# Four heads' numerators in four adjacent PSUM banks, one multiply for qT, whole loads, and stores placed behind loads

## The chip, the cores and the metric

The kernel runs on one core of one Trainium2 chip. The metric is the time of one execution in microseconds (us) on the device; lower is better. A program on one core gives runs that differ by one to two per cent, so each comparison below ran both kernels in the same rounds on the same chip. A run counts as fast unless it is over 1.5% above the fastest run of its own kernel. The profiles are of single executions; times in them are us from the start of the span.

## The reference, cut to what matters

```python
q_p = phi(q)              # relu(q) * cos and relu(q) * sin, side by side: 64 -> 128 features
k_p = phi(k)
kv  = einsum('bhsf,bhsd->bhfd', k_p, v);   z = sum(k_p, axis=2)
num = einsum('bhsf,bhfd->bhsd', q_p, kv);  den = einsum('bhsf,bhf->bhs', q_p, z)[..., None] + 1e-06
x   = num / den                            # 8 batches, 8 heads, 576 positions, 64 wide; heads joined to 512
wq, wk = x @ w_q, x @ w_k                  # 512 -> 64
mixed  = (wq @ wk.T / 8) @ x
out    = relu(mixed) @ w_out               # fp32, 8 x 576 x 512
```

## The kernel before

Heads are worked in 16 groups of four (H = 0 to 15), two groups to a batch. For each group TensorE does `qT` (transposes of relu(q)), `kv`, `num` (numerator, with the denominator as a 65th column) and `xT` (transposes of x). For each batch it does `wqk`, `wk`, `kx` and four `mx`. For each pair of batches it does nine row tiles `wo` of the output, each copied out by `oe` and stored by `st` in five stores of one or two tiles. VectorE multiplies k by cos and sin (`mk`, line 392), does the qT multiply (`qe`, line 420) and the division (`norm`). POOL does most of the ReLUs and casts of inputs (`rq`, `rk`, `rv`). `plan_order` simulates the engines once on the host and fixes the order of all operations; each engine then works in that order, and so does each queue that issues transfers. The plan also holds TensorE back once in every 256 of its instructions, and longer when the transfers are behind (the variables `left_in` and `block`).

```python
def norm(H, r, m):                       # twice for a group: r = 0, 1
    nv = bank(m, 2)[:, :, 0:SC * (D + 1)].rearrange("p t (u e) -> p t u e", u=SC)
    ...
    nc.vector.reciprocal(rec, nv[:, :, :, D:D + 1])
    ...
    nc.vector.tensor_tensor(xv[:, h, r], nv[:, :, :, 0:D], rec.to_broadcast([P, 2, SC, D]), op=ALU.mult)
...
def qT_evac(H, r, m):                    # twice for a group
    nc.vector.tensor_mul(qpt_bufs[H % 2][:, r, :, D:SLOTS * D],
        bank_h(m)[:, 0:1, 0:HC].to_broadcast([P, 2, HC]), cst)
...
CS = ((0, 5), (5, C9))                   # a tile of inputs is loaded in two parts
    if kind == "load":
        load(j, parts=CS, names=(b,))
    ...
    elif kind == "st":                   # a store is two transfers, each of 64 partitions
        last = b == B // 2 - 1 and j >= 2
        store(b, j, (nc.sync, A if last else nc.sync))
...
for n, eng, m in plan_order(NB):
    emit(n, eng, m)
```

## Time and profile before

| | before |
|---|---|
| time, median of three runs (range) | 130.08 us (130.00 to 131.48) |
| span of the profiled run | 129.5 us (this run measured 131.6) |
| busy: TensorE, VectorE, ScalarE, POOL | 102.7, 95.0, 79.6, 71.1 us |
| first row tile starts, last copy ends | 44.3, 123.75 us |
| qT multiply of group 4, of group 15 starts | 28.4, 102.8 us |

The costliest rows of VectorE on the page (source line, engine, operation, output <- inputs, partitions x elements and type, count | busy us, mean ns of one | idle us just before, and what ended it) give the price of what is merged:

```profile
L466 DVE TENSOR_TENSOR x_sb<-ps,rec 128x640 bf16<-128x640 f32 x32 | 26.4, 825 | 1.1
L420 DVE TENSOR_TENSOR qpt_buf<-ps,cst 128x1152 bf16<-128x1152 bf16 x32 | 22.7, 750 | 1.7 <-PE ps L414 1.7
```

Thirty-two divisions of 640 elements and thirty-two qT multiplies of 1152 are 49.1 of VectorE's 95.0 us.

### The profile page before, as it was taken

The page shows a single profiled execution, that of the slowest core. Times are in us where ns is not written, and L with a number is a line of the kernel's source. Part 1 is how long each engine was busy: PE and PEld are TensorE (multiplying, and loading weights), DVE is VectorE, ACT ScalarE, POOL GpSimd, SP SyncE. Part 2 cuts the span into 40 slices and gives each one's busy share as a digit, 9 for nine tenths or more (in the row PEclk, how much of TensorE's full clock was granted, in tenths as well). Part 3 has the DMA queues.
Part 4 walks back from the last instruction along what each step waited for, and adds up shares of the span by engine and source line. Part 5 has one row for each costly group of instructions (what it writes and reads, how often), then busy time and mean ns, then how long its engine had stood idle before and what let it go on. Part 6 is the DMA issues. An engine that isn't in the chain of part 4 may idle for free.

```text
span 129.5 us, 5391 instructions
## 1 busy us (share of the span) xinstructions
PE 102.7 (79%) x2262; PEld 63.3 (49%) x2286; DVE 95.0 (73%) x156; ACT 79.6 (61%) x155; POOL 71.1 (55%) x113
## 2 busy tenths in 40 slices
PE   5957694757498998979997878998886999998900
PEld 2334353545375644646664645555564655543400
DVE  1067878999789999899989596999899688314000
ACT  6959435083705677687688755864766376656710
POOL 7720557568489999897289287876652710000000
PEclk9999999999756999999999999999999999999995
DMA  3999999999999999999999999999999754667893
GB/s 86 369 359 357 359 309 354 340 337 383 365 356 358 356 358 366 376 378 369 340 356 360 332 308 379 351 347 323 316 318 326 266 133 123 164 166 189 202 210 128
DMA packets 32968, 39.41 MB, mean 304 GB/s; under 512 B 3248, under 2 KB 27824, under 8 KB 32944
## 3 DMA queue, kind: packets, MB, share of 16 engines
q1 hardware_dynamic: 32304, 38.09, 90.9%
q10 hardware_dynamic: 640, 0.98, 2.6%
q8 instruction: 18, 0.29, 0.9%
q14 instruction: 6, 0.05, 0.1%
HBM read 29.62 MB, written 9.44 MB: 302 GB/s over the span
## 4 chain that ended last, share of the span: by engine, by line
PE 47%; DMA 19%; DVE 16%; issue 7%; ACT 3%; POOL 2%; SPq 1%; POOLq 0%
PE ps L563 20%; DMA raw<-in_k_dram 8%; PE ps L493 6%; DMA raw<-in_v_dram 6%; PE ps L453 4%; DVE qpt_buf L420 4%; PE ps L428 4%; DVE x_sb L466 4%; DMA raw<-in_q_dram 4%; DVE kp L392 3%; PE ps L478 3%; PE ps L523 3%; PE ps L539 2%; PE ps L414 2%; POOL rq_buf L379 2%
## 5 line engine op out<-in xcount | busy, mean ns | idle before, releaser
L563 PE MATMUL ps<-wo_sb,mix_sb 128*128 128x512 bf16 x126 | 34.4, 380 | 2.8 <-DVE xT_buf L368 0.9
L379 POOL TENSOR_SCALAR rq_buf<-raw 128x640 bf16<-128x640 f32 (+1 forms) x30 | 26.2, 887 | 16.9 <-DMA raw<-in_q_dram 13.5
L366 ACT COPY o_sb<-ps 128x512 f32<-128x512 f32 x36 | 21.1, 586 | 12.4 <-PE ps L563 11.0
L392 DVE TENSOR_TENSOR kp<-rk,cossin 128x2304 bf16<-128x2304 bf16 (+2 forms) x17 | 23.0, 1352 | 7.8 <-ACT rk L377 6.1
L466 DVE TENSOR_TENSOR x_sb<-ps,rec 128x640 bf16<-128x640 f32 x32 | 26.4, 825 | 1.1
L404 POOL TENSOR_SCALAR v_buf<-raw 128x640 bf16<-128x640 f32 (+1 forms) x26 | 22.5, 879 | 6.2 <-DMA raw<-in_v_dram 3.0
L420 DVE TENSOR_TENSOR qpt_buf<-ps,cst 128x1152 bf16<-128x1152 bf16 x32 | 22.7, 750 | 1.7 <-PE ps L414 1.7
L379 POOL TENSOR_SCALAR rk<-raw 128x640 bf16<-128x640 f32 (+1 forms) x28 | 18.3, 668 | 8.8 <-DMA raw<-in_k_dram 6.2
L563 PEld LDWEIGHTS <-mix_sb 128*128 128x128 bf16 x144 | 12.2, 97 | 14.5 <-issue 2.4
L428 PE MATMUL ps<-v_buf,kp 64*128 64x65 bf16 x576 | 13.1, 193 | 5.7 <-ACT v_buf L402 2.2
L428 PEld LDWEIGHTS <-kp 64*128 64x128 bf16 x576 | 11.1, 95 | 9.5 <-DVE kp L392 5.0
L453 PE MATMUL ps<-kv_sh,qpt_buf 64*128 64x65 bf16 x320 | 14.5, 193 | 1.2 <-issue 1.2
L551 ACT ACTIVATE mix_sb<-ps 128x576 bf16<-128x576 f32 x24 | 14.5, 655 | 1.4 <-PE ps L539 1.3
L453 PEld LDWEIGHTS <-qpt_buf 64*128 64x128 bf16 x640 | 12.9, 96 | 4.9 <-issue 3.9
L453 PE MATMUL ps<-kv_sb,qpt_buf 64*128 64x65 bf16 x320 | 14.5, 194 | 0.1
L368 DVE COPY xT_buf<-ps 128x640 bf16<-128x640 bf16 (+1 forms) x19 | 8.4, 456 | 6.1 <-PE ps L478 3.9
L289 PE MATMUL ps<-warm 128*128 128x512 bf16 x32 | 11.2, 487 | 1.8 <-DVE warm L285 1.5
L414 PE MATMUL ps<-ident,rq_buf 64*128 64x64 bf16 x288 | 8.3, 193 | 3.3 <-POOL rq_buf L379 1.8
L366 ACT CAST wT_buf<-ps 128x576 bf16<-128x576 f32 x8 | 5.1, 637 | 8.2 <-PE ps L493 8.2
L493 PE MATMUL ps<-xT_buf,wqk_sb 128*128 128x288 bf16 x64 | 10.1, 306 | 0.0
L366 ACT CAST kv_sb<-ps 128x260 bf16<-128x260 f32 x15 | 5.6, 375 | 6.9 <-PE ps L428 5.7
L478 PE MATMUL ps<-ident,x_sb 64*128 64x64 bf16 x288 | 7.6, 190 | 2.3 <-DVE x_sb L466 1.5
(51 smaller groups left out, 123.1 us busy)
## 6 DMA issues: line engine op xcount, KB each, us to landing
out_dram<-o_sb SPq DMA_DIRECT2D x30, 256.0 KB, 5.2
raw<-in_q_dram SPq DMA_DIRECT2D x16, 320.0 KB, 6.0
raw<-in_v_dram SPq DMA_DIRECT2D x16, 320.0 KB, 6.2
raw<-in_k_dram SPq DMA_DIRECT2D x15, 320.0 KB, 5.8
raw<-in_q_dram SPq DMA_DIRECT2D x16, 256.0 KB, 5.9
raw<-in_k_dram SPq DMA_DIRECT2D x16, 256.0 KB, 6.0
raw<-in_v_dram SPq DMA_DIRECT2D x16, 256.0 KB, 6.3
wo_f<-in_moe_w_out_dram SPq DMA_DIRECT2D x1, 1024.0 KB, 8.1
```

Source lines behind the costliest of these rows:

```text
L366: nc.scalar.copy(dst, src)
L379: eng.tensor_scalar(dst, src, FMAX, 0.0, op0=ALU.min, op1=ALU.max)
L392: nc.vector.tensor_mul(kp[H][:, 2 * lo:2 * hi], rks[H][:, lo:hi].rearrange("p c i d -> p (c i) d").unsqueeze(2) .to_broadcast([P, 2 * (hi ...
L404: eng.tensor_scalar(dst, src, 1.0, 1.0, op0=ALU.mult, op1=ALU.mult)
L420: nc.vector.tensor_mul(qpt_bufs[H % 2][:, r, :, D:SLOTS * D], bank_h(m)[:, 0:1, 0:HC].to_broadcast([P, 2, HC]), cst)
L428: nc.tensor.matmul(bank(m + r)[:, 0, i * (D + 1):(i + 1) * (D + 1)], kp[H][half_rows(r), 2 * c + i, :, :], v_bufs[H % 3][half_rows(r), c, ...
L453: nc.tensor.matmul(nb[t][:, u, :], qpt_bufs[H % 2][rows, r, w, u * P:(u + 1) * P], mv, start=(u == 0 and w == 0), stop=False)
L466: nc.vector.tensor_tensor(xv[:, h, r], nv[:, :, :, 0:D], rec.to_broadcast([P, 2, SC, D]), op=ALU.mult)
L478: nc.tensor.transpose(bank_h(m + r)[:, 0, k0 * D:(k0 + 1) * D], xs[b][half_rows(r), u, 2 * hp:2 * hp + 2, :], ident[half_rows(r), half_row ...
L493: nc.tensor.matmul(bank(m + nh)[:, 0, 0:hs], wqk_sb[:, dmc, :, :], xT_bufs[b % 2][:, dmc, nh * hs:(nh + 1) * hs], start=(dmc == 0), stop=( ...
L551: nc.scalar.activation(dst, src, AF.Relu, scale=scale_moe)
L563: nc.tensor.matmul(bank(m)[:, 0, :], mixs[bp][:, dmc, rt * P:(rt + 1) * P], wo_sb[:, dmc, :], start=(dmc == 0), stop=(dmc == NDM - 1))
```

## The change

Its intent: fewer and longer operations on VectorE, longer runs in the loads, stores that do not stand in front of loads, and more output buffers (12 for 5) so that row tiles never wait for a store. `plan_order` got new weights, so the whole order of the program moved too. The term `ds` puts every store 15 us later in the plan's list of transfers, and the last four row tiles are stored with their copies. The core of the diff, with cuts marked:

```diff
-PLAN = dict(mk=1.3, pa=7.848, ... wo_at=4, nraw=6, nout=5, ...)
+PLAN = dict(mk=1.3, pa=7.189, ... wo_at=3, nraw=6, nout=12, ... ds=15)
...
-                    key = t
+                    key = t + (par["ds"] if n[0] == "st" else 0)
...
-        for r in range(2):
-            op(("num", H, r), {"PE": .33}, [("kve", H), ("qe", H, r), ...], pa, "row", 2)
-            op(("norm", H, r), {"DVE": 1.0}, [("num", H, r)], 2, ...)
+        op(("num", H), {"PE": .68}, [("kve", H), ("qe", H), ...], par["pn"], "row", 4)
+        op(("norm", H), {"DVE": 1.68}, [("num", H)], par["pno"], ...)
...
-            qpt_bufs[H % 2][:, r, :, D:SLOTS * D],
-            bank_h(m)[:, 0:1, 0:HC].to_broadcast([P, 2, HC]), cst)
+            qpt_bufs[H % 2][:, :, :, D:SLOTS * D],
+            bank_h(m, 2)[:, :, 0:HC].unsqueeze(2).to_broadcast([P, 2, 2, HC]),
+            cst.unsqueeze(1).to_broadcast([P, 2, 2, HC]))
...
-    def norm(H, r, m):
+    def norm(H, m):
...
-        rec = small.tile([P, 2, SC, 1], FP32, name="rec")
+        rec = small.tile([P, 4, SC, 1], FP32, name="rec")
         nc.vector.reciprocal(rec, nv[:, :, :, D:D + 1])
...
-            xv[:, h, r], nv[:, :, :, 0:D], rec.to_broadcast([P, 2, SC, D]), op=ALU.mult)
+            xv[:, h], nv[:, :, :, 0:D], rec.to_broadcast([P, 4, SC, D]), op=ALU.mult)
...
-            load(j, parts=CS, names=(b,))
+            load(j, names=(b,))
...
             wout_evac(b, j, m, engs[eng])
+            if b == B // 2 - 1 and j > 4:
+                lo = (j - 5) % 2
+                store(b, (j + 1) // 2, (nc.sync, A), lo, lo + 1)
         elif kind == "st":
-            last = b == B // 2 - 1 and j >= 2
-            store(b, j, (nc.sync, A if last else nc.sync))
+            if b < B // 2 - 1 or j < 3:
+                store(b, j, (nc.sync, nc.sync))
```

More of the change, by code (lines that the diff above doesn't have):

```diff
@@ L22 @@
 EPS_HI = 9.9837780e-07
-PLAN = dict(mk=1.3, pa=7.848, pc=8.447, pm=8.738, pw=6.677, pb=0.821, flex=0.189, poe=11.845,
-            pme=34.049, pmk=1108.864, wo_at=4, nraw=6, nout=5, sw=0, amp=0, seed=99119,
-            sl=0.1, bd=0.2, pact=1)
+PLAN = dict(mk=1.3, pa=7.189, pc=7.595, pm=3.84, pw=4.572, pb=0.65, flex=0.147, poe=3714.738,
+            pme=7.206, pmk=16.167, wo_at=3, nraw=6, nout=12, sw=0, amp=0, seed=19615,
+            sl=0.05, bd=0.3, pact=1, pqe=92.894, pno=0.978, pn=7.389, res=0, ds=15)
 PAIRS = ((0, 1), (2, 3), (4,), (5, 6), (7, 8))
-PE_COUNT = dict(qT=36, kv=72, num=44, xT=36, wqk=16, wk=10, kx=20, mx=4, wo=8)
+PE_COUNT = dict(qT=36, kv=72, num=88, xT=36, wqk=16, wk=10, kx=20, mx=4, wo=8)
 def plan_order(NB, par=None):
@@ L48, in ago @@
         return name if cond else None
-    prep = {"POOL": 1.37, "ACT": 1.1} if par["pact"] else {"POOL": 1.37}
+    prep = {"POOL": 1.37, "ACT": 1.1}
     pa, pc, pm, pw = par["pa"], par["pc"], par["pm"], par["pw"]
@@ L63, in plan_order @@
                par["pmk"])
-        op(("qT", H), {"PE": .26}, [ago(H, "rq", H), ago(H, "kv", H - 1),
-                                    ago(H > 1, "num", H - 2, 1)], pa, "row", 2)
-        for r in range(2):
-            op(("qe", H, r), {"DVE": .67}, [("qT", H)], 3,
-               frees=(("qT", H), r))
+        op(("qT", H), {"PE": .26}, [ago(H, "rq", H), ago(H > 1, "num", H - 2)], pa, "row", 2)
+        op(("qe", H), {"DVE": 1.31}, [("qT", H)], par["pqe"], frees=(("qT", H), None))
         op(("kv", H), {"PE": .58}, [ago(H, "mk", H), ago(H, "rv", H),
-                                    ago(H > 2, "num", H - 3, 1)], pa, "row", 2)
+                                    ago(H > 2, "num", H - 3)], pa, "row", 2)
         op(("kve", H), {"ACT": .96, "DVE": 1.1}, [("kv", H)], 3,
            frees=(("kv", H), None))
-        for r in range(2):
-            op(("num", H, r), {"PE": .33}, [("kve", H), ("qe", H, r),
-                                        ago(b > 2, "kx", b - 3)], pa, "row", 2)
-            op(("norm", H, r), {"DVE": 1.0}, [("num", H, r)], 2,
-               frees=(("num", H, r), None))
-        op(("xT", H), {"PE": .24}, [("norm", H, 0), ("norm", H, 1),
-                                    ago(b > 1, "wqk", b - 2)], pc, "row", 2)
+        op(("num", H), {"PE": .68}, [("kve", H), ("qe", H), ago(b > 2, "kx", b - 3)],
+           par["pn"], "row", 4)
+        op(("norm", H), {"DVE": 1.68}, [("num", H)], par["pno"],
+           frees=(("num", H), None))
+        op(("xT", H), {"PE": .24}, [("norm", H), ago(b > 1, "wqk", b - 2)], pc, "row", 2)
         op(("xe", H, 0), {"ACT": .49, "DVE": .35}, [("xT", H)], 2, frees=(("xT", H), 0))
@@ L88, in plan_order @@
            frees=(("wqk", b), None))
-        op(("wqc", b), {"DVE": .36}, [("we", b)], 1)
+        op(("wqc", b), {"ACT": .57, "DVE": .36}, [("we", b)], 1)
         op(("wk", b), {"PE": .14}, [("we", b)], pc, "row", 1)
@@ L140, in plan_order @@
     while ready:
-        best = None
+        best, held = None, ()
+        for n in ready:
+            if ops[n]["banks"] == 4 and par["res"]:
+                u = min((0, 2, 4), key=lambda u: (sum(x > 1e8 for x in bank[u:u + 4]),
+                                                  max(bank[u:u + 4])))
+                held = range(u, u + 4)
         for n, t in ready.items():
@@ L151, in plan_order @@
                     s = max(free[e] + (.1 if o["mode"] != mode else 0), t)
-                    if o["banks"] == 2:
-                        u = min((0, 2, 4, 6), key=lambda i: max(bank[i], bank[i + 1]))
-                        s, mine = max(s, bank[u], bank[u + 1]), (u, u + 1)
-                    elif o["banks"] == 1:
-                        s = max(s, min(bank))
-                        u = max((i for i in range(8) if bank[i] <= s),
-                                key=lambda i: bank[i ^ 1])
-                        mine = (u,)
+                    w = o["banks"]
+                    where = [u for u in ((0, 2, 4) if w == 4 else range(0, 8, w))
+                             if w == 4 or u not in held]
+                    s = max(s, min(max(bank[u:u + w]) for u in where))
+                    u = max((u for u in where if max(bank[u:u + w]) <= s),
+                            key=lambda u: (bank[u ^ 1] if w == 1 else 0,
+                                           bank[(u ^ 2) & 6], u))
+                    mine = tuple(range(u, u + w))
                     key = s - .1 * o["prio"] + (par["sw"] if o["mode"] != mode else 0)
                 elif e == "DMA":
-                    key = t
+                    key = t + (par["ds"] if n[0] == "st" else 0)
                 elif len(o["cost"]) > 1:
@@ L417, in qT_mm, with qT_evac @@
                     ident[half_rows(r), half_rows(r)])
-    def qT_evac(H, r, m):
+    def qT_evac(H, m):
         nc.vector.tensor_mul(
-            qpt_bufs[H % 2][:, r, :, D:SLOTS * D],
-            bank_h(m)[:, 0:1, 0:HC].to_broadcast([P, 2, HC]), cst)
+            qpt_bufs[H % 2][:, :, :, D:SLOTS * D],
+            bank_h(m, 2)[:, :, 0:HC].unsqueeze(2).to_broadcast([P, 2, 2, HC]),
+            cst.unsqueeze(1).to_broadcast([P, 2, 2, HC]))
     def kv_mm(H, m):
@@ L441, in kv_evac, with num_mm @@
         kvs[H] = (kv_sb, kv_sh)
-    def num_mm(H, r, m):
-        nb = [bank(m + t)[:, 0, 0:SC * (D + 1)].rearrange(
-            "p (u e) -> p u e", u=SC) for t in range(2)]
+    def num_mm(H, m):
+        nb = [bank(m + j)[:, 0, 0:SC * (D + 1)].rearrange(
+            "p (u e) -> p u e", u=SC) for j in range(4)]
         kv_sb, kv_sh = kvs[H]
-        for u in range(SC):
-            for w in range(2):
-                for t in range(2):
-                    rows = half_rows(t)
-                    mv = (kv_sb[rows, r, t * (D + 1):(t + 1) * (D + 1)] if w == 0
-                          else kv_sh[rows, r, :])
-                    nc.tensor.matmul(
-                        nb[t][:, u, :], qpt_bufs[H % 2][rows, r, w, u * P:(u + 1) * P],
-                        mv, start=(u == 0 and w == 0), stop=False)
-        for t in range(2):
-            nc.tensor.matmul(nb[t][:, :, D], ones_t[half_rows(t), :],
-                             eps_t[half_rows(t), :], start=False, stop=True)
@@ L460, in norm @@
-    def norm(H, r, m):
+        for r in range(2):
+            for u in range(SC):
+                for w in range(2):
+                    for t in range(2):
+                        rows = half_rows(t)
+                        mv = (kv_sb[rows, r, t * (D + 1):(t + 1) * (D + 1)] if w == 0
+                              else kv_sh[rows, r, :])
+                        nc.tensor.matmul(
+                            nb[2 * t + r][:, u, :],
+                            qpt_bufs[H % 2][rows, r, w, u * P:(u + 1) * P],
+                            mv, start=(u == 0 and w == 0), stop=False)
@@ L461, in norm @@
+        for r in range(2):
+            for t in range(2):
+                nc.tensor.matmul(nb[2 * t + r][:, :, D], ones_t[half_rows(t), :],
+                                 eps_t[half_rows(t), :], start=False, stop=True)
+    def norm(H, m):
         b, h = divmod(H, 2)
-        nv = bank(m, 2)[:, :, 0:SC * (D + 1)].rearrange("p t (u e) -> p t u e", u=SC)
-        rec = small.tile([P, 2, SC, 1], FP32, name="rec")
+        nv = bank(m, 4)[:, :, 0:SC * (D + 1)].rearrange("p j (u e) -> p j u e", u=SC)
+        rec = small.tile([P, 4, SC, 1], FP32, name="rec")
@@ L464, in norm @@
         nc.vector.reciprocal(rec, nv[:, :, :, D:D + 1])
-        xv = xs[b].rearrange("p u (h t r) d -> p h r t u d", h=2, r=2)
+        xv = xs[b].rearrange("p u (h j) d -> p h j u d", h=2)
         nc.vector.tensor_tensor(
-            xv[:, h, r], nv[:, :, :, 0:D], rec.to_broadcast([P, 2, SC, D]), op=ALU.mult)
+            xv[:, h], nv[:, :, :, 0:D], rec.to_broadcast([P, 4, SC, D]), op=ALU.mult)
     def xT_mm(H, m):
@@ L500, in wqk_evac, with wq_copy @@
              bank(m, 2)[:, :, 0:hs])
-    def wq_copy(b):
+    def wq_copy(b, eng):
         wq2 = moe.tile([P, S], BF16, name="wq2")
-        nc.vector.tensor_copy(wq2[64:128], wT_bufs[b % 2][0:64, D:SLOTS * D])
+        copy(eng, wq2[64:128], wT_bufs[b % 2][0:64, D:SLOTS * D])
         wqTs[b] = wq2
@@ L571, in wout_evac, with store @@
         copy(eng, o_sbs[bp, g][:, rt - PAIRS[g][0], :], bank(m)[:, 0, :])
-    def store(bp, g, qs):
-        n = len(PAIRS[g])
-        for hi in range(2):
-            qs[hi].dma_start(
-                dataclasses.replace(out, offset=out.offset + out_dest(bp, PAIRS[g][0], hi),
-                                    ap=[[C9 * DM, 64], [2 * DM, n], [1, DM]]),
-                o_sbs[bp, g][64 * hi:64 * hi + 64, 0:n, :])
+    def store(bp, g, qs, lo=0, hi=2):
+        rts = PAIRS[g][lo:hi]
+        for half in range(2):
+            rows = slice(64 * half, 64 * half + 64)
+            qs[half].dma_start(
+                dataclasses.replace(out, offset=out.offset + out_dest(bp, rts[0], half),
+                                    ap=[[C9 * DM, 64], [2 * DM, len(rts)], [1, DM]]),
+                o_sbs[bp, g][rows, lo:lo + len(rts), :])
     A, V, G = nc.scalar, nc.vector, nc.gpsimd
@@ L604, in emit @@
         elif kind == "qe":
-            qT_evac(b, j, m)
+            qT_evac(b, m)
         elif kind == "kv":
@@ L610, in emit @@
         elif kind == "num":
-            num_mm(b, j, m)
+            num_mm(b, m)
         elif kind == "norm":
@@ L614, in emit @@
                 xs[b // 2] = xpool.tile([P, SC, NH, D], BF16, name="x_sb")
-            norm(b, j, m)
+            norm(b, m)
         elif kind == "xT":
@@ L624, in emit @@
         elif kind == "wqc":
-            wq_copy(b)
+            wq_copy(b, engs[eng])
         elif kind == "wk":
```

## The prediction

> **What bounds the kernel now.** I read the page's slices first, to see which engine is full when.
>
> ```profile
> PE   5957694757498998979997878998886999998900
> DVE  1067878999789999899989596999899688314000
> PEclk9999999999756999999999999999999999999995
> DMA  3999999999999999999999999999999754667893
> GB/s 86 369 359 357 359 309 354 340 337 383 365 356 358 356 358 366 376 378 369 340 356 360 332 308 379 351 347 323 316 318 326 266 133 123 164 166 189 202 210 128
> ```
>
> A slice is 3.24 us. The DMA engines are full from slice 1 to slice 30 (3 to 100 us) at about 355 GB/s. VectorE is at nine tenths from about 23 to 94 us. TensorE is half idle in the first third and at nine tenths after it. So the first 45 us are a problem of supply (loads, then VectorE), and the rest one of TensorE. The chain of waits agrees: up to 26.6 us it names only loads, from 28 to 62 us mostly VectorE, then TensorE almost alone. Its end:
>
> ```profile
> 113.92 0.65 PE ps L563 x3
> 114.57 0.25 PE ps L509 x5
> 114.82 0.97 PE ps L563 x4
> ...
> 118.66 4.49 PE ps L563 x20
> ...
> 123.17 0.58 ACT o_sb L366
> ```
>
> A row tile of the output product (line 563, four matmuls) costs 0.97 us. The last copy ends at 123.75 us, and the last store takes until 129.5, a tail of 5.75 us. The first output product starts at 44.34 us (timeline of TensorE).
>
> I then weighed the work left on TensorE. Costs in us, read between starts in full-clock stretches of chain and timeline: for each group of four heads (H, 16 of them) qT .33, kv .65, num .69, xT .27; for each batch (8) wqk .98, wk .20, kx .67, the four mx .52; for each row tile (36) .97. That is 16 x 1.94 + 8 x 2.37 + 36 x .97 = 84.9 us. In program order seven qT, six kv, six num, five xT, two wqk/wk/kx and one mx precede the first row tile: 15.9 us. The other 69.0 us took from 44.34 to 123.15, 78.8 us: TensorE runs at **88%** once it has work. So the end is set by when the row tiles begin and by that 88%.
>
> Two more views give the prices. VectorE's timeline (start, duration):
>
> ```profile
> 54.65 0.21 DVE L464 RECIPROCAL rec<-ps 128x10 f32<-128x10 f32 x1
> 54.89 0.82 DVE L466 TENSOR_TENSOR x_sb<-ps,rec 128x640 bf16<-128x640 f32 x1
> 55.63 1.35 DVE L392 TENSOR_TENSOR kp<-rk,cossin 128x2304 bf16<-128x2304 bf16 x1
> 56.90 1.42 DVE L420 TENSOR_TENSOR qpt_buf<-ps,cst 128x1152 bf16<-128x1152 bf16 x2
> 58.23 0.21 DVE L464 RECIPROCAL rec<-ps 128x10 f32<-128x10 f32 x1
> ```
>
> Instructions overlap a little, so I price start to start: reciprocal .24, multiply of 640 .74, kp multiply of 2304 bf16 1.27, two of 1152 together 1.33. Windows of 1 us, the last column GB/s:
>
> ```profile
> 30.00:31.00 1.00, 1.00 (x11) 0.52 (x11) 1.00 (x1) 0.48 (x1) 1.00 (x1) 1.00 1.04 391
> 31.00:32.00 1.00, 0.23 (x15) 0.32 (x17) 0.97 (x3) 0.00 (x0) 1.00 (x2) 1.00 1.04 391
> ...
> 46.00:47.00 1.00, 1.00 (x39) 0.74 (x38) 1.00 (x3) 0.59 (x1) 1.00 (x2) 1.00 1.11 361
> ```
>
> At 30 to 32 us the weight matrix with rows of 2048 B is moving (issued 25.0, landed 33.1); at 46 us input loads in runs of 1280 and 1024 B. Both are saturated; the longer runs give 391 against 361.
>
> **What the Trainium skill says.** "DMA: Bandwidth & Descriptors", section "Why small descriptors are slow (HBM only)", gives each packet a fixed overhead; the 391 against about 358 agrees. "VectorE: DVE Perf Modes", section "Rules for kernel authors", says to minimise the count of operations; its section on the errata puts a fixed cost on each instruction. Here that cost is small: 1.33 against 1.27 us, some .06. "PSUM — Partial Sum Buffer", section "PSUM bank collisions raise a hardware error", forbids two engines in one bank at a time; so four banks written together come back only after the merged multiply. No wait in this trace is labelled as one for a bank.
>
> **The change, part by part.**
>
> *Loads.* 45 of 48 input tiles become one transfer with runs of 2304 B. If a packet costs a + b x bytes on one of 16 engines, a pair of 1280 + 1024 B at 358 GB/s takes 103.0 ns and 2048 B at 391 takes 83.8 ns; then a is about 10 ns, and 2304 B take 93.0 ns, or 396 GB/s (estimate). A tile of .59 MB takes 1.49 us in place of 1.65: 45 x .16 = 7.1 us of DMA time. Start 2.5 us, first three tiles 4.9, 45 tiles 67.1, weights 3.4 and the 3.7 MB of stores still ahead of the last load 9.4 put the last load at about 87 us, against about 101.5 before. Against it: ReLU on the first part of a tile waits for all of it, under .8 us, once where supply is short.
>
> *Output weights one group earlier, and the new order.* The first row tile now stands after five qT, four kv, three num, three xT and one each of wqk, wk, kx, mx: 9.5 us of TensorE work instead of 15.9. It waits for the q load of group 4, which 8.4 MB precede: 2.5 + 4.9 + (8.98 - 1.77) MB / .393 = 25.8 us. With POOL's ReLU (1.4), qT and small waits the first row tile starts at about **28.5 us**.
>
> *VectorE.* The multiply of 1280 is 2 x .74 - .06 = 1.42, one reciprocal .25: 1.67 for 1.96, saving .29. qT in one multiply of 2304: 1.27 for 1.33. Together .35 x 16 = 5.6 us. Moved away by the program's new order: 2 xT copies (.45 each), 3 mix copies (.75), 5 wq copies (.53), 3 small ones (.33); one output copy (.6) comes: another 6.2 us. VectorE goes from 95 to about 83 us busy, from 5.9 to 5.2 us a group. ScalarE gains about 5.5 (to 85), POOL about 1.8 (to 73). None is then above TensorE's 5.3 us a group of pure work, and none of this is on the path by itself: it is what lets the 88% hold earlier.
>
> *TensorE.* No matmul is added or removed; warm-up matmuls go from 38 to 33 by the order.
>
> *Stores.* 12 output buffers for 5 free the row tiles from waiting for stores. The last transfers are one row tile (.26 MB) and not two (.52 MB): at the 200 GB/s of the last slices 1.3 us off the tail, leaving 4.5.
>
> **Sum.** 84.9 - 9.5 = 75.4 us of work from 28.5 us on. At 88% it takes 85.7 us: 114.2; last copy .6, tail 4.5: 119.3 us of span. The measured time was .6 over the profiled span (130.08 against 129.5): 119.9. With VectorE and DMA less full I allow 90%: 118.0. I choose **119.0 us**.
>
> Check against the end of the inputs: the last load at 87 us and 3.3 us of preparation let the last kv start at 90.5; from it to the last copy lies a serial chain of about 16 us (kv .7, its copies .9, num .7, norm 1.7, xT .3, copy .6, wqk 1, copy .65, wk .2, copy .4, kx .7, copy .4, mx and its copy .8, five row tiles 4.9, about .1 for each of a dozen hand-overs). That gives 112 at the earliest, so TensorE and not the supply sets the end.
>
> **Rivals.**
>
> 1. *Supply stays the bound.* For it: the DMA is full for 97 us, and even at 355 GB/s the bytes before the last load explain only about 95 of the 101.5 us, so some 6 us go to a queue that stops, and a store in front of a load can still stop it. Against it: the longer runs, and stores placed later. With the old rate and the old 6 us: last load 101.6, plus 3.3 + 16 + 5 + .6: 126.5 us.
>
> 2. *PSUM becomes the bound.* A num holds four of eight banks for about .7 + .1 + 1.7 = 2.5 us, or 10 bank-us a group, where two halves held some 6. For all uses I estimate 30 of the 45 bank-us that a period of 5.6 us has. If TensorE falls to 82% through it: 28.5 + 92 + 5.1 + .6 = 126 us. Against it: the num period stays above twice the 2.5 us.
>
> 3. *The merge delays more than it saves.* num must wait for the whole qT multiply (1.27, not .67), and xT for the whole norm; in the last serial chain that is about a microsecond. Alone it would cost 1 to 2 us, not the gain.
>
> 4. *It goes better.* TensorE at 93%: 115 us.
>
> **Range and chances.** 88% carries most of the uncertainty: one point is 1 us. 86% with a late start gives 122.5, and a partial stall of rival 1 or 2 about 124; 93% gives 115. So 114.5 to 124 eight times in ten. For less than 2% gained both the early start and the faster loads would have to fail: 6%; a loss of 2% would need a new wait of 12 us: 1%.
>
> **What would show it.** In the profile after: input loads at 385 GB/s or more, the last one landed by 92 us; the first row tile at 27 to 31 us; multiplies of 1280 at about 1.5 us and of 2304 at 1.35 us duration, 16 each; VectorE near 83 us busy; TensorE at nine tenths from 30 us on; under 5 us from last copy to end. The prediction is wrong if the row tiles start early but TensorE then shows holes behind norm (rival 2), or if the loads keep 355 GB/s and TensorE goes on waiting for them (rival 1).

## The result, and the profile after

The changed kernel takes **140.23 us** (median of 139.55, 140.25 and 140.23), against 130.08: a loss where a gain of 8.5% was predicted. The ratio is 1.0724, with a 95% interval of 1.063 to 1.0817. All ratios here are the mean time of one kernel's fast runs over that of the other's of the same rounds, so they are not quite the ratio of the medians quoted.

The slices of the changed kernel's page, to be laid beside those of before in the prediction (one digit for each slice, 3.45 us here; tenths busy, the granted clock of TensorE, and the rate of the transfers):

```profile
PE   5967796897988789859888889889899999880000
DVE  1164995979697978857977858696979750400000
PEclk9999999569999999999999999999999999997555
DMA  4999999999999999999999999942480000038893
GB/s 106 371 387 391 353 348 354 399 394 395 389 390 391 390 397 401 406 387 406 396 403 405 395 406 399 410 170 59 118 202 15 5 2 0 5 85 227 255 299 124
```

Three things are to be seen. The loads run at 387 to 410 GB/s from 24 us on and are over near 90 us: this part came as predicted. From slice 30 to 34, counted from 0, some 103 to 121 us, nothing moves at all (15, 5, 2, 0, 5 GB/s), and then the stores come in a heap after TensorE has finished. And TensorE, in the row PE, has many 7s and 8s between 30 and 80 us where before had more 9s.

VectorE's rows answer to those of before:

```profile
L420 DVE TENSOR_TENSOR qpt_buf<-ps,cst 128x2304 bf16<-128x2304 bf16 x16 | 21.7, 1354 | 5.9 <-PE ps L414 5.5
L470 DVE TENSOR_TENSOR x_sb<-ps,rec 128x1280 bf16<-128x1280 f32 x16 | 23.9, 1491 | 0.5
```

The merged operations cost what was predicted (1491 and 1354 ns), and VectorE fell from 95.0 to 86.1 us busy. But VectorE now waits 5.9 us ahead of the qT multiply, for TensorE's transposes, where it waited 1.7.

The end of the chain of waits after (start, us, what), and the waits of the sync engine's queue, which issues nearly all transfers (who waits <- for whom: us in total, times, longest):

```profile
122.13 0.59 ACT o_sb L366
122.72 0.02 issue
122.75 0.50 ACTq L581
...
124.52 0.58 ACT o_sb L366
```

```profile
SPq L581 <- ACT o_sb L366: 25.9, 7, 19.2
```

The last copy of a row tile ends at 125.1 us, where before ended at 123.75; so the compute part gained nothing. Between the last copies ScalarE now issues half of a store (.50 us on its queue), which sets the copies about 1.2 us apart. After the last one comes a tail of 12.7 us, where before had 5.75. The second fence says why: one store stood in the sync queue for 19.2 us waiting for its copy. The order of that queue, read from the program (`st.2.3` is store 3 of the third pair of batches, `[oe.3.5]` the store of row tile 5 of the last pair, issued with its copy), is

```
... load.v.15 st.1.3 st.1.4 st.2.0 st.2.1 st.2.2 [oe.3.5] [oe.3.6] [oe.3.7] [oe.3.8] st.2.3 st.2.4 st.3.0 st.3.1 st.3.2
```

The plan puts every `st` 15 us late, but the last four row tiles are stored outside the plan, with their copies. So five stores of nine finished row tiles (2.4 MB) stand behind row tile 5 of the last pair, whose copy is done only at 121.5 us. These 2.4 MB and the last four tiles' 1.0 MB then had the 16.3 us from 121.5 us to the end, on average 209 GB/s.

How the groups follow each other is the other half of the comparison (starts on the timelines, us):

| kernel | first row tile | qT multiply, group 4 | group 15 | last copy ends | span |
|---|---|---|---|---|---|
| before | 44.3 | 28.4 | 102.8 | 123.75 | 129.5 |
| after | 32.2 | 31.7 | 101.9 | 125.1 | 137.8 |

The row tiles begin 12 us earlier, and the last group comes at about the same time. From its qT multiply to the last copy it takes 21.0 us before and 23.2 us after. The groups do follow each other faster, 6.4 us apart from group 4 to group 15 where before had 6.8, but group 4 itself comes 3.3 us later. In the order of the loads the 1.05 MB of output weights now stand ahead of the inputs of group 4 and no longer behind them; at some 390 GB/s that is 2.7 us (an estimate; no run moved the weights back).

### The profile page after: what moved, and what is told of

Read it like the earlier page. It is cut to its first block, busy times and chain, and to the rows that moved or that the text cites. A ratio compares the mean times of both kernels' runs of the same rounds, so it can differ in the third digit from the quotient of the medians.

```text
span 137.8 us, 5264 instructions
## 1 busy us (share of the span) xinstructions
PE 104.6 (76%) x2281; PEld 61.9 (45%) x2281; DVE 86.1 (63%) x97; ACT 84.6 (61%) x165; POOL 67.3 (49%) x115
## 4 chain that ended last, share of the span: by engine, by line
PE 49%; DVE 15%; DMA 10%; ACT 6%; issue 5%; SPq 2%; POOL 2%; ACTq 1%; DVEq 0%; POOLq 0%
PE ps L567 18%; PE ps L429 6%; PE ps L455 6%; DMA raw<-in_q_dram 6%; PE ps L497 6%; DVE x_sb L470 5%; DMA raw<-in_v_dram 4%; PE ps L527 4%; DVE qpt_buf L420 4%; PE ps L482 4%; ACT o_sb L366 3%; POOL rq_buf L379 2%; PE ps L414 2%; PE ps L543 2%; DVE kp L392 2%
## 5 line engine op out<-in xcount | busy, mean ns | idle before, releaser
L567 PE MATMUL ps<-wo_sb,mix_sb 128*128 128x512 bf16 x144 | 36.0, 380 | 4.4 <-ACT mix_sb L555 2.4
L379 POOL TENSOR_SCALAR rq_buf<-raw 128x640 bf16<-128x640 f32 (+1 forms) x30 | 22.4, 764 | 13.3 <-DMA raw<-in_q_dram 11.5
L420 DVE TENSOR_TENSOR qpt_buf<-ps,cst 128x2304 bf16<-128x2304 bf16 x16 | 21.7, 1354 | 5.9 <-PE ps L414 5.5
L379 POOL TENSOR_SCALAR rk<-raw 128x640 bf16<-128x640 f32 (+1 forms) x28 | 19.2, 704 | 10.5 <-DVE kp L392 10.1
L470 DVE TENSOR_TENSOR x_sb<-ps,rec 128x1280 bf16<-128x1280 f32 x16 | 23.9, 1491 | 0.5
L555 ACT ACTIVATE mix_sb<-ps 128x576 bf16<-128x576 f32 x27 | 16.7, 652 | 4.6 <-PE ps L543 4.5
L455 PE MATMUL ps<-kv_sb,qpt_buf 64*128 64x65 bf16 x320 | 13.6, 195 | 1.5 <-issue 0.7
L455 PEld LDWEIGHTS <-qpt_buf 64*128 64x128 bf16 x640 | 11.6, 96 | 6.6 <-issue 5.2
L455 PE MATMUL ps<-kv_sh,qpt_buf 64*128 64x65 bf16 x320 | 12.9, 193 | 0.0
L366 ACT COPY xT_buf<-ps 128x512 bf16<-128x512 bf16 (+1 forms) x15 | 9.0, 617 | 1.8 <-PE ps L482 1.7
L497 PE MATMUL ps<-xT_buf,wqk_sb 128*128 128x288 bf16 x64 | 9.8, 299 | 0.0
L543 PE MATMUL ps<-wT_buf,kx 64*128 64x288 bf16 x32 | 7.6, 293 | 2.2 <-DVE mix_sb L557 1.0
```

Of the source, the lines that this page charges most:

```text
L366: nc.scalar.copy(dst, src)
L379: eng.tensor_scalar(dst, src, FMAX, 0.0, op0=ALU.min, op1=ALU.max)
L420: nc.vector.tensor_mul(qpt_bufs[H % 2][:, :, :, D:SLOTS * D], bank_h(m, 2)[:, :, 0:HC].unsqueeze(2).to_broadcast([P, 2, 2, HC]), cst.unsqu ...
L455: nc.tensor.matmul(nb[2 * t + r][:, u, :], qpt_bufs[H % 2][rows, r, w, u * P:(u + 1) * P], mv, start=(u == 0 and w == 0), stop=False)
L470: nc.vector.tensor_tensor(xv[:, h], nv[:, :, :, 0:D], rec.to_broadcast([P, 4, SC, D]), op=ALU.mult)
L497: nc.tensor.matmul(bank(m + nh)[:, 0, 0:hs], wqk_sb[:, dmc, :, :], xT_bufs[b % 2][:, dmc, nh * hs:(nh + 1) * hs], start=(dmc == 0), stop=( ...
```

## The experiments

Two theories stood after the comparison. **Store order**: the misplaced stores cost the tail, about 7 us. **Closed loop**: VectorE works in a fixed order and waits for TensorE twice in each group (for xT and for qT), so a faster VectorE waits longer and the period of about 6 us stays. The rivals were **supply** (the transfers set the pace, as the prediction had it) and **TensorE's own order**. The letter a stands for kernels made from the changed one, b for kernels made from the one before. Below, a bare number such as 1.0239 is the ratio to the kernel before of the same rounds.

### First batch: stores and loads

**a_flush**: each of the five stores is issued when its last copy is out (`st.2.3` one copy later).

```diff
+    early = {("oe", 2, 7): ("st", 2, 3), ("oe", 2, 8): ("st", 2, 4), ("oe", 3, 1): ("st", 3, 0),
+             ("oe", 3, 3): ("st", 3, 1), ("oe", 3, 4): ("st", 3, 2)}
     for n, eng, m in plan_order(NB):
-        emit(n, eng, m)
+        if n not in early.values():
+            emit(n, eng, m)
+        if n in early:
+            emit(early[n], "DMA", None)
```

> The changed kernel with only the place of five stores moved: those of row tiles 5 to 8 of the third pair and 0 to 4 of the last pair are issued as soon as their copies are, ahead of the stores of the last four row tiles. Theory A (the sync queue stood behind the stores of the last row tiles while nine finished row tiles waited): the DMA engines work between 102 and 120 us, the last copy stays at about 125 us, the tail after it falls from 12.7 to about 4 us, and the time from 140.2 to 131 us (129.5 to 132.5). Rival B (the end is bound by the rate of stores, whatever their order): 138 us or more.

134.45 us, 1.0239 (1.0124 to 1.0354): 5.8 us of the loss were the order of five stores. It did not reach the 131 expected because `st.2.3` now stood ahead of `st.2.0` to `st.2.2` and blocked those until 108.9 us.

**a_flush_sp**: also the second half of each late store on the sync queue, not on ScalarE's.

```diff
-                store(b, (j + 1) // 2, (nc.sync, A), lo, lo + 1)
+                store(b, (j + 1) // 2, (nc.sync, nc.sync), lo, lo + 1)
```

> The same, and the second half of each of the last four stores is issued by the sync queue and not by ScalarE. If ScalarE's 0.5 us issues between the last copies delay them (the copies stand 1.25 us apart in the changed kernel, 0.86 in the kernel before), the last copy comes 1.3 us earlier and the time is about 1 to 1.5 us below a_flush. If the extra issues on the sync queue cost as much at the end: within 0.5 us of a_flush.

134.49 us, 1.0301 (1.0222 to 1.0379). The copies moved together, from about 1.2 to .86 us apart, and the last one ended at 124.9 us, not 126.6. But the sync queue still had stores to issue, one in about .6 us until 129.9 us, so nothing was gained.

**b_whole**: the kernel before with whole loads and nothing else.

```diff
-            load(j, parts=CS, names=(b,))
+            load(j, names=(b,))
```

> The kernel before with whole loads and nothing else. If the supply of inputs bounds the first 60 us (my prediction's reading), 396 in place of 358 GB/s brings 3 to 5 us: 125 to 127 us. If the first 60 us are bound by the loop between VectorE and TensorE (qT multiply, kp multiply, norm, xT and qT again, some 6 us for a group in both kernels), it stays within 1%: 129 to 131 us.

131.6 us, 1.0068 (0.9976 to 1.0161). The rate rose to 390 to 400 GB/s over most of the loads and the time did not fall. (TensorE waited 2.1 us longer for no semaphore, see the fourth batch, which may hide part of a gain, but not the 3 to 5 us expected.) The theory of supply loses here for the first time.

**a_flush_parts**: a_flush with its loads in two parts again (the same line, the other way).

> a_flush with the loads in two parts again, as in the kernel before. If supply matters in the changed kernel, it is 4 to 6 us slower than a_flush (the last load lands at about 97 us in place of 89). If the loop between VectorE and TensorE sets the pace, within 1.5 us of a_flush, though the loads come later.

131.8 us, 1.011 (1.0042 to 1.0178): 2.6 us better than a_flush by the medians. So whole loads did not just fail to help in the changed kernel, they cost.

### Second batch: the right store order, and the loop

**a_nat_parts**: split loads; after the last load every store follows its last copy, in order; of the last row tiles only the very last one's second half goes through ScalarE (a_flush_sp has shown that such a change of queue gains nothing by itself).

```diff
-            load(j, names=(b,))
+            load(j, parts=CS, names=(b,))
-                store(b, (j + 1) // 2, (nc.sync, A), lo, lo + 1)
+                store(b, (j + 1) // 2, (nc.sync, A if j == 8 else nc.sync), lo, lo + 1)
...
+    last = max(i for i, (n, _, _) in enumerate(order) if n[0] == "load")
+    ends = {(p, g): ("oe", p, rts[-1]) for p in range(B // 2) for g, rts in enumerate(PAIRS)}
...
+        if i >= last:                        # stores left over: each when its last copy is out
+            for st in sorted(late):
+                if ends[st[1:]] in seen: ... emit(st, "DMA", None)
```

> The changed kernel with its loads split in two again and, from the last load on, every store issued directly after its last copy, in the order of the row tiles (last row tiles on the sync queue, only the second half of the very last one on ScalarE). Theory (store order): the run with five stores moved (131.8 us) still had the transfers idle before 110 us and a tail of 7 us, so with the whole order right the tail falls to 4 to 5 us at an unchanged last copy of about 122: 127 to 128.5 us. Rival (the stores' own rate of 200 to 300 GB/s bounds the end, wherever they are issued): 131 us or more.

129.21 us, 0.9822 (0.9745 to 0.9899), with a last copy at 121.6 and a tail of 5.6 us. Against a_flush_parts (1.011) the right order is worth another 2.9%. The rival (a rate of 200 to 300 GB/s bounds the end anyway) is out.

**a_nat**: the same with whole loads, so the changed kernel with only the store order mended.

> a_nat_parts with whole loads, as the change has them: the change with nothing but the store order mended. Theory (whole loads cost, as in the pair with five stores moved: 134.45 against 131.8): 129.5 to 131.5 us, 2 to 3 us above a_nat_parts, with more issue time on TensorE. Rival (the 2.6 us were an accident of where the half clock and the stores fell): within 1 us of a_nat_parts.

132.2 us, 1.0032 (0.9943 to 1.0122). The store order alone takes the change from 1.0724 to 1.0032; whole loads against split ones cost 2.1% a second time.

**a_nat_parts_mk**: VectorE's multiply of k and POOL's ReLU of k earlier in the order, to fill VectorE's waits.

```diff
+    for H in range(2, NB):
+        ...
+        if order[at("rk", H)][1] == "POOL":
+            move("rk", [("rq", H), ("mk", H - 2), ("load", "k", H)])
+        move("mk", [("rk", H), ("norm", H - 2), ("kv", H - 2)])
```

> The same, and for every group H from 2 on VectorE's multiply of k (L392, 1.27 us) and POOL's ReLU of k are put earlier in the order: ahead of the xT copies and of the qT multiply of that group, not after them. Theory (closed loop): VectorE, in program order, loses .56 us waiting for xT and .41 us waiting for qT in each period of 6.0 us; with mk in that place it has 1.27 us of work to do there, the period falls to 5.4 to 5.6 us over some 8 to 10 groups, and the time lies 3 to 5 us under a_nat_parts. Rival (TensorE or the loads set the period of 6 us): within 1 us of a_nat_parts.

138.23 us, 1.0468 (1.0352 to 1.0583): a clear miss. The waits of TensorE (who <- for whom: us in total, times, longest) and VectorE's timeline of this kernel say why:

```profile
PE ps L497 <- DVE xT_buf L368: 3.5, 3, 2.4
...
PE ps L455 <- DVE qpt_buf L420: 1.5, 3, 1.2
```

```profile
58.58 1.35 DVE L392 TENSOR_TENSOR kp<-rk,cossin 128x2304 bf16<-128x2304 bf16 x1
59.85 1.35 DVE L420 TENSOR_TENSOR qpt_buf<-ps,cst 128x2304 bf16<-128x2304 bf16 x1
```

In the order of seven of the groups the multiply of k now stands ahead of a copy of xT, and `wqk` (L497) waits up to 2.4 us for one. In all of them it stands ahead of the qT multiply, as the timeline shows for group 8. The next `num` (L455) needs four adjacent banks, two of which hold that qT; its first matmul starts at 59.87 us, the second at 61.25, when the qT multiply is done: the wait of 1.2. The profile also has three stretches of half clock, 17 us together, before the tail. With `mk` behind `qe`, as it was, the banks would come free about 1.3 us earlier (the price of `mk`; an estimate).

**a_nat_parts_norm2**: the norm in two again, over the same four banks.

```diff
-        nc.vector.reciprocal(rec, nv[:, :, :, D:D + 1])
...
+        for j in (0, 2):
+            nc.vector.reciprocal(rec[:, j:j + 2], nv[:, j:j + 2, :, D:D + 1])
+            nc.vector.tensor_tensor(xv[:, h, j:j + 2], nv[:, j:j + 2, :, 0:D], ...)
```

> a_nat_parts with the merged norm cut in two again (two reciprocals, two multiplies of 640 for four heads, over the same four banks). It costs VectorE about .3 us a group. Closed loop theory: the norm is in the loop, so 16 x .3, of which some 10 count: +2.5 to +4 us. If VectorE's work doesn't bound: within 1 us. (If the merged multiply is what delays xT, nothing gets better either, since xT waits for both halves.)

132.77 us, 1.0097 (1.0007 to 1.0187), so 3.6 us slower, as the loop wants it. But the profile has 3.7 us in which TensorE waits for no semaphore, and that of a_nat_parts only .5.

### Third batch: qT, and what is wrong with whole loads

**a_nat_parts_qt** and **a_nat_qt**: qT earlier in TensorE's order, where no bank stands against it; with split and with whole loads. The rule moves nine groups in the plan's list. For eight of them TensorE's order changes: qT goes ahead of one xT, kv or mx, but that of group 9 ahead of mx, a row tile, wqk and num.

```diff
+    for H in range(2, NB):
+        at = next(i for i, it in enumerate(order) if it[0] == ("qT", H))
+        ...                                  # back to the first op that shares a bank or a buffer
+        order.insert(to, order.pop(at))
```

> a_nat_parts with qT of nine of the groups moved earlier in TensorE's order, ahead of the xT or kv in front of it, where the banks allow; nothing moves on VectorE. Closed loop (VectorE loses .41 us a group waiting for qT): up to .4 us in each of those groups, 1 to 3 us under a_nat_parts. Rival (with split loads the supply sets the 6 us: POOL waits 17.6 us for loads there): within 1 us.

> The same with whole loads, where POOL hardly waits for loads (3 us) and VectorE waits 7.3 us for qT. Closed loop: 2 to 3.5 us under a_nat, so about 129. Rival (what TensorE loses there are waits that no semaphore explains, 3.3 us of issue): within 1 us of a_nat, 132.

132.85 us, 1.0168 (1.0089 to 1.0247), and 132.91 us, 1.0101 (1.0002 to 1.02). From 30 us on, VectorE's wait for qT fell, from 4.1 to 2.1 us with split and from 7.3 to 1.2 us with whole loads, and its waits for xT rose, from 6.5 to 7.7 and from 7.2 to 10.3. The wait moved and the time did not fall; with split loads it rose by 3.5%, which I cannot explain (the long move of group 9 is one suspect, not tested). The closed loop in the form that I had given it has fallen, with this and with the run before.

**a_nat_halves**: whole loads, each as two transfers of 64 partitions.

```diff
+                for ph in (slice(0, 64), slice(64, P)) if (lo, hi) == (0, C9) else (slice(0, P),):
-                eng.dma_start(raw[nm, H][:, :, lo * D:hi * D], srcs[nm][b][:, h0:h0 + 2, ...])
+                    eng.dma_start(raw[nm, H][ph, :, lo * D:hi * D], srcs[nm][b][ph, h0:h0 + 2, ...])
```

> a_nat with each load of a tile as two transfers of 64 partitions, still in runs of 2304 B: the packets and the rate of whole loads, the number of transfers of split ones. If the 3 us between a_nat and a_nat_parts come from the size of the transfer (each .59 MB), this gives 129 to 130 us; if from the longer packets or from inputs that come early, 131.5 to 133.

156.72 us, 1.2003 (1.1859 to 1.2148): neither of the two. The same 10 us of a_nat and of this kernel, as windows (start and end, length, busy us and count for PE, PEld, DVE, ACT and POOL, clock, share of the transfer engines, GB/s):

```profile
50.00:60.00 10.00, 8.60 (x229) 5.61 (x231) 7.13 (x9) 6.69 (x16) 8.94 (x13) 1.00 1.05 401
```

```profile
50.00:60.00 10.00, 7.82 (x251) 5.74 (x244) 6.85 (x9) 6.15 (x14) 5.72 (x9) 1.00 1.04 245
```

The engines are as full as before (1.04), at 245 GB/s and not 401. The Trainium skill, "SBUF — State Buffer", section "Door 1: The DMA port swizzle", says that 64 neighbouring partitions reach only 8 of the 16 ports of the memory; the trace agrees in kind. I had not looked it up before I planned this run. It spoils the run for its purpose, and it shows what supply looks like when it does bind. It also raised a question: every store of all these kernels is a transfer of 64 partitions.

**a_nat_parts_qe2**: the qT multiply in two again.

```diff
+        for r in range(2):
+            nc.vector.tensor_mul(qpt_bufs[H % 2][:, r, :, D:SLOTS * D],
+                bank_h(m + r)[:, 0:1, 0:HC].to_broadcast([P, 2, HC]), cst)
```

> a_nat_parts with the qT multiply in two again (two of 1152). From the profile of before it costs VectorE .06 us a group: within 1 us of a_nat_parts, so at most +1 us; nothing hangs on the merge of qT.

129.91 us, 0.9872 (0.978 to 0.9963), against 0.9822: nothing that can be told apart from zero, as expected.

### Fourth batch: fetches, stores, clock

In most of these profiles TensorE stands still now and then for no semaphore; the profile labels it issue. The trace also has a queue of transfers that bring instructions: 18 of 16 KB in each run. I measured each such stand of .25 us or more against the start of the latest instruction transfer, over the profiles of all kernels: there are 62, and every one ends 2.24 to 2.85 us after such a start (median 2.47). A transfer begins only about every 6 us, so this is no accident: these are waits for instructions. All that the profile labels issue, the shorter stands too, adds up over a run to

| loads | TensorE waiting for no semaphore, us |
|---|---|
| whole | after 3.3, a_flush 4.2, a_flush_sp 2.0, b_whole 5.9, a_nat 4.3, a_nat_qt 1.9 |
| two parts | before 3.8, b_w128 1.7, a_flush_parts .8, a_nat_parts .5, a_nat_parts_mk 0, a_nat_parts_norm2 3.7, a_nat_parts_qe2 1.9, a_nat_parts_qt 0, a_nat_parts_w128 3.9, a_nat_parts_warm 2.2 |
| each whole load in two transfers | a_nat_halves 6.8, a_nat_pr 0, a_nat_pr_warm 2.2, a_nat_pr_warm_norm2 2.0 |

This leans one way but is no proof, so it was tested. (Some of the runs listed come only below.)

**a_nat_pr**: whole rows of 2304 B over all 128 partitions, but in two transfers of half the length (one for each of the two rows that a partition holds).

```diff
+                for i in range(2) if (lo, hi) == (0, C9) else (slice(0, 2),):
+                    j = slice(i, i + 1) if isinstance(i, int) else i
-                eng.dma_start(raw[nm, H][:, :, lo * D:hi * D], srcs[nm][b][:, h0:h0 + 2, ...])
+                    eng.dma_start(raw[nm, H][:, j, lo * D:hi * D],
+                                  srcs[nm][b][:, h0 + j.start:h0 + j.stop, ...])
```

> a_nat with each whole load as two transfers of 128 partitions, one for each of the two rows of a partition: runs of 2304 B as before, each transfer half as long. If TensorE's unexplained waits come from fetches of its instructions that stand behind long transfers of loads (the Trainium skill, DMA: Bandwidth & Descriptors, section Queues, rings and completion order, has the engines change queues only between packets): issue waits of TensorE fall from 3.3 us to under 1 us and the time to 129 to 130.5. If the cause is the early supply or the order that follows from it: 131.5 to 133, as a_nat.

128.84 us, 0.9739 (0.9647 to 0.983), from two fast runs of four (all four: 126.85 to 129.9). Waits of TensorE from 30 to 128 us, first in a_nat, then here (both profiles fell on runs counted as slow by the 1.5% rule, so like is laid beside like):

```profile
PE ps L567 <- ACT mix_sb L555: 2.4, 5, 0.6
PE ps L429 <- issue: 1.6, 2, 1.0
...
PE ps L414 <- issue: 0.9, 1, 0.9
```

```profile
PE ps L569 <- ACT mix_sb L557: 2.4, 5, 0.6
PE ps L484 <- DVE x_sb L472: 1.3, 3, 0.6
PE ps L416 <- POOL rq_buf L381: 0.8, 1, 0.8
```

No issue wait is left in this profile, and the 3 us are back. So each whole load in two transfers along its rows is about 3 us better than in one; that is shown. Why is not. Three things speak against length alone. The rate changed with it: from 30 to 80 us a_nat moved 393 GB/s, a_nat_pr 364 and a_nat_parts 351, so the early supply that the expectation named as the rival is not held fixed. a_nat_halves, also with transfers of .29 MB, has 6.8 us of such waits. And a_nat_parts_w128 and a_nat_parts_warm (both below) have 3.9 and 2.2 us of them, where a_nat_parts has .5, at times within 1.1 us of its own. The Trainium skill, "DMA: Bandwidth & Descriptors", section "Queues, rings and completion order", says that each transfer engine takes turns between queues only at whole packets; a fetch of instructions behind more of a load's data would then start later. No view here shows a packet's turn, and what the profile itself lists as packets of these loads is 2304 B in both runs, so this last link is argued and not shown.

**a_nat_parts_w128** and **b_w128**: each store as one transfer of 128 partitions. Their outputs are wrong, which doesn't matter for the times.

```diff
-        for half in range(2):
-            rows = slice(64 * half, 64 * half + 64)
-            qs[half].dma_start(..., o_sbs[bp, g][rows, lo:lo + len(rts), :])
+        qs[0].dma_start(
+            dataclasses.replace(out, offset=out.offset + row0 * DM,
+                                ap=[[C9 * DM, P], [2 * DM, len(rts)], [1, DM]]),
+            o_sbs[bp, g][:, lo:lo + len(rts), :])
```

> Wrong rows on purpose: every store of a_nat_parts as one transfer of 128 partitions to other rows of the same size and spacing, where the right result needs two of 64. Runs of 64 partitions moved at 220 to 270 GB/s in a_nat_halves, against 390. Stores then take some 24 us of transfer time in place of some 43. If supply still bounds the middle: 3 to 5 us less, and the last load lands about 7 us earlier. If TensorE's order does: only the tail gains, about 1 us.

> The same in the kernel before, wrong rows on purpose too. Prediction on record: before, the first 45 us are supply. No store lies in those, so the start doesn't change; if supply bounds the later part too, 4 us or more below 130; if TensorE does, within 1.5 us.

130.22 us, 0.9937 (0.9865 to 1.001), and 130.81 us, 0.997 (0.9898 to 1.0043). The last loads were issued by 90.5 us where a_nat_parts had 95.7, and by 92.8 us where before had 96.4: supply came 5.2 and 3.6 us earlier, and the time did not fall. For the kernel before this says that supply does not bound its second half: b_w128 even has fewer of the waits for instructions (1.7 us for 3.8). In a_nat_parts_w128 they rose from .5 to 3.9 us and may have hidden a gain, so for the changed kernel it is less sure.

**a_nat_parts_warm**: six idle matmuls ahead of qT of group 4, to keep TensorE's clock up.

```diff
+        if n == ("qT", 4):
+            warm_up(6, 7)
```

> a_nat_parts with six matmuls more on a free bank just ahead of qT of group 4, where TensorE stood idle for 1.9 us before a stretch of 3.4 us at half clock. If the idle time is what brings the half clock: no stretch at half clock before the tail, the first row tile 1 to 2 us earlier, and the time 0.5 to 1.7 us below a_nat_parts. Rival (the slack is lost again in the middle): within .5 us.

129.12 us, 0.9848 (0.9789 to 0.9907), against 0.9822. In the profile the half clock before the tail was gone (granted clock .997 over the span, .97 without; of the four runs without, one has .993 as well, at no better time), the first row tile came at 31.3 us and not at 32.2, and the time was the same: the rival was right.

### Fifth batch: the merged norm once more, and the best version

**a_nat_pr_warm** is a_nat_pr with those six matmuls. **a_nat_pr_warm_norm2** is the same with the norm in two, by the edit shown above.

> a_nat_pr (whole rows, two transfers a tile, stores in order) with the six matmuls that kept the clock up in a_nat_parts_warm. a_nat_pr measured 0.974 of the kernel before; the clock changed nothing by itself in a_nat_parts: 0.965 to 0.98, some 126 to 128.5 us, faster than the kernel before by over 2%.

> The same with the norm in two (two reciprocals, two multiplies of 640), which costs VectorE about .3 us a group. If VectorE's norm lies on the path in the middle: 2.5 to 4 us above a_nat_pr_warm. If the 3.6 us that this split cost before were the late fetches: within 1 us.

129.71 us, 0.9793 (0.9709 to 0.9876), and 130.28 us, 0.9924 (0.9865 to 0.9983). The fast runs have means of 127.9 and 129.8. The difference of the fast runs, 1.9 us, lies between the two expectations; the medians of all six runs differ by .6 us only. TensorE's waits, without and with the split:

```profile
PE ps L484 <- DVE x_sb L472: 2.1, 4, 1.1
```

```profile
PE ps L486 <- DVE x_sb L473: 4.1, 9, 0.9
```

TensorE's transposes of x wait 2.0 us longer for the split norm, and the profiled spans differ by 2.1 us (127.7 against 125.6). So the merge gains about 2 us in fast runs. a_nat_pr_warm and a_nat_pr are the best versions found, 2.1 and 2.6% faster than the kernel before by their fast runs (three of six and two of four). Both intervals reach below 2%, so the verdict on each is unclear. They keep both merges and the plan, and mend stores and loads.

## Why the prediction was wrong, point by point

By the profiled run (139.55 us) the prediction's own sum, 118.0 at 90%, is 21.5 us short. Its terms against the trace:

| step | predicted | measured | short by |
|---|---|---|---|
| first row tile | 28.5 us | 32.2 | 3.7 |
| 75.4 us of work on TensorE | 83.8 us, at 90% | 91.3 (32.2 to 123.4), 83% | 7.5 |
| last copy starts after TensorE's end | 0 us | 1.1 (copies held up by ScalarE's issues) | 1.1 |
| tail after the last copy | 4.5 us | 12.7 | 8.2 |
| measured time over span | .6 us | 1.75 | 1.1 |

- **Loads: right as a rate, wrong in its sign.** 396 GB/s was predicted, 387 to 410 came from 24 us on, and the last load was issued at 82.8 us and landed near 90, where 87 was predicted. The step's 45 x .16 = 7.1 us of DMA time was about right for the transfers and worth nothing to the kernel (b_whole), and the whole loads cost about 3 us against the same rows in two transfers (a_nat against a_nat_pr), whatever the reason. Nor does the length of a run alone give the rate, as the step had it: a_nat_pr has the same runs of 2304 B and moved 364 GB/s.
- **VectorE: right.** Multiplies of 1491 and 1354 ns and 86 us busy, against some 1.5, 1.35 and 83 (it counted five copies of wq as moved to ScalarE; the program moves four). Of the 16 x .29 = 4.6 us that the merged norm saves on VectorE, about 2 reach the time (fifth batch). The merged qT multiply gives nothing that can be measured (a_nat_parts_qe2).
- **Stores: failed.** The step read "The last transfers are one row tile (.26 MB) and not two (.52 MB)". It took the stores to be issued as their tiles are done and did not read the order of the sync queue, although the order of the changed program could be read. The order cost 7% (1.0724 to 1.0032).
- **First row tile: off in size, and without weight.** The step let the q load of group 4 land at 25.8 us; POOL's ReLU waited for it until 28.55, which is 2.7 of the 3.7 us. From 13.8 to 24.1 us the transfers ran at 348 to 354 GB/s and not at the 393 of the step. TensorE also ran at half clock from 23.5 to 30.3 us, where the step counted its work at full clock. Taking away such a stretch (a_nat_parts_warm) moved the row tile by 1 us and not the end.
- **The bound: failed, and most of the lost gain lies here.** The step was "So the end is set by when the row tiles begin and by that 88%". Row tiles began 12 us earlier and the last group's qT multiply came .9 us earlier. Before group 15 the row tiles are filling: TensorE does them in the gaps of the groups. The 88% came from a stretch of before in which work was nearly always waiting, and was carried to one in which it was not. By the same prices the changed kernel reached 83%. The loss lies between 40 and 80 us, as these windows show (start and end, length, PE busy us and count, clock, share of the transfer engines, GB/s), first before, then after:

```profile
40.00:50.00 10.00, 8.96 (x227) 0.95 1.08 357
50.00:60.00 10.00, 9.03 (x246) 1.00 1.06 374
60.00:70.00 10.00, 9.09 (x244) 1.00 1.03 357
70.00:80.00 10.00, 8.49 (x209) 1.00 1.00 332
```

```profile
40.00:50.00 10.00, 7.55 (x236) 1.00 1.05 392
50.00:60.00 10.00, 8.71 (x209) 1.00 1.05 400
60.00:70.00 10.00, 8.66 (x231) 1.00 1.05 399
70.00:80.00 10.00, 7.55 (x190) 1.00 1.05 402
```

  That is 35.6 against 32.5 us busy, while the loads ran faster after than before; from 80 to 120 us it is 36.0 against 36.7. No one wait fills the holes: from 32 us on TensorE waits 4.0 us for copies of the mixed tiles, 3.3 us for no semaphore, 1.6 us for qT multiplies and 1.3 us for norm, where before, from 44 us on, waited 2.0, 3.5, 0 and .6. In every profile here 21 to 23 us lie between the qT multiply of the last group and the last copy, so the end came when the last group came, plus that; this is a regularity of the runs and no experiment moved the last group alone.
- **Rival 1, supply: fell** for the later part (b_whole, b_w128; with less weight a_nat_parts_w128), except for one clause of it, "a store in front of a load"; it was a store in front of a store. **Rival 2, PSUM:** its figure of 82% is what came, within a point, but its cause was not tested: the waits just named for norm and qT are 2.9 us in all, and a_nat_parts_mk shows that the four banks can make TensorE wait, 1.2 us there at one time. **Rival 3, the merge delays:** not supported, since the split norm is the slower one; but there each half still waits for the whole num over four banks, so the delay that it meant was only in part taken away.

What stays open: why the groups still come about 6.1 us apart (31.9 to 99.4 us for eleven groups in a_nat_parts), with TensorE nine tenths busy over most of that, and what a_nat_parts_qt lost. Waits moved from one place to another in every run that changed the order, so I name no single bound there.

## What to carry to other kernels

Read the order of the queue that issues the stores, not only the order of the compute: a store issued with its copy, in a queue planned otherwise, can hold up everything behind it. Do not carry an engine's efficiency from a stretch where work was always waiting to one where it was not; ask first which arrival sets the end. And when transfers are made longer, look afterwards for waits that no semaphore explains: instructions travel on the same engines, and here the same rows in two transfers were 3 us better than in one, at a lower rate.

## What the Trainium skill lacked or had wrong

- "DMA: Bandwidth & Descriptors" advises large transfers and describes turns at packets, but does not say that TensorE can stand still for its own instructions while such loads run. "Runtime: NRT & Kernel Launch", section "Instruction fetch mechanics", has the blocks of 16 KiB, but calls the cost of crossing into the next one mostly hidden. Here it is not always: 62 stands of .25 us or more in these profiles, each ending 2.24 to 2.85 us after an instruction transfer began, and from 0 to 6.8 us of such waits in a run.
- "SBUF — State Buffer", section "Door 1: The DMA port swizzle", is borne out in kind by 64-partition loads, though they ran at 245 GB/s over 10 us where its table gives an asymptote of about 218 (the two halves of a tile reach different ports, so some overlap may explain that; not examined), and 401 where it has 436 for 128 partitions. Stores of 64 partitions cost no time here that could be measured (0.997 for b_w128 without them).
- "TensorE: Matmul & The Clock Gate", section "Part 1: The HAM clock gate", has half clock come after at least one idle window of about 3.4 us. Stretches of 3.4 and 6.8 us of half clock are in these traces, but in the two that were looked at the 3.41 us ahead were only partly idle: TensorE was busy for 2.07 us of them in the changed kernel and for 1.47 us in a_nat_parts.
